# Routing by six digits of the key in place of five, in a fused attention, mixture and expert kernel

## The chip, the cores and the metric

The kernel runs on one core of one Trainium2 chip. The metric is the device time of one execution in microseconds (us); lower is better. A core has five engines that run their own instruction queues in order: TensorE (PE in the rows; PEld is its weight loading), VectorE (DVE), ScalarE (ACT), GpSimd (POOL) and SyncE (SP), which issues most of the transfers. They meet at semaphores.

## The reference

Three stages follow each other. The first is windowed attention with four sink keys (4 batches, 8 heads, 768 positions). The second takes the 3072 tokens by 512 features, multiplies them by three weights, takes the largest of the three elementwise, and multiplies by an output weight. The third gives each token to one of eight experts:

```python
cap = N // E                              # 3072 // 8 = 384
logits = x @ w_gate                       # [3072, 8]
order = np.argsort(-logits.flatten())
for idx in order:                         # greedy, best bid first
    tok, e = (int(idx) // E, int(idx) % E)
    if assigned[tok] >= 0 or counts[e] >= cap:
        continue
    assigned[tok] = e
    counts[e] += 1
for e in range(E):
    mask = assigned == e
    out[mask] = np.maximum(x[mask] @ w1[e], 0.0) @ w2[e]
```

## The kernel before

Attention and the second stage run in eight groups of 384 tokens, and the second stage's matmuls (L295, L317) fill TensorE to about 665 us. Then the eight experts are computed one after another, in the order in which the routing closes them: each has 96 matmuls of 384 columns for the first layer (L604, hidden tile `mm`) and 72 of 512 columns for the second (L597, `acc`). Every weight is split into a high and a low part first: ScalarE copies the high part (L549, `wah`, `wbh`), VectorE or GpSimd subtracts for the low one (L551, `wbl`, `wal`). L608 does the same for the hidden activations on VectorE (`hl`).

Routing is the class `Route`. The greedy loop is done in at most seven phases: in each phase every unassigned token bids for its best open expert, and the phase ends when one expert becomes full. It looks for the bid value at which that happens. The bids become 32-bit integer keys whose order is that of the bids (L418, L419), and the value is found digit by digit, from the top, with a tree of counts. `SH` holds the shift of each digit and `NZ` the number of values that it can have. One pass of the loop below is called a level here.

```python
for l in range(n):
    k=s.NZ[l]
    if l==0: pc=s.pc
    else:
        pc=s.ps.tile([128,512],FT,name="rc")
        s.count(pc,s.compare(z,k,OP.is_ge),k)
    w=s.t([128,24],FT,"w")
    if l<n-1: V.scalar_tensor_tensor(w,z[:,:,0],128.0,DS[:,l,:],op0=OP.mult,op1=OP.add)
    V.tensor_scalar(met[0:M,0:k],pc[0:M,0:k],s.RP[0:M],None,op0=OP.is_ge)
    nc.tensor.matmul(v[:,0:k],s.scale[0:M],met[0:M,0:k],start=True,stop=True)
    V.tensor_scalar(hit[:,1:k],v[:,1:k],128.0,None,op0=OP.min,op1=OP.add,accum_out=d)
    V.tensor_scalar(z,w[:,:,None].to_broadcast([128,24,2]),d,None,op0=OP.subtract)
```

`compare` (L398, tile `th`) holds the digit of each of the 3072 tokens (24 columns on 128 partitions) against the k thresholds, 24 times k results in bf16 on VectorE. `count` (L404) sums them per expert on TensorE: 24 matmuls, each with its own 128x128 weight load from the one-hot bids (`ohr`) and k moving columns. `met` (L448) asks which counts exceed the expert's room, one matmul with `scaleb` (L450) spreads that over all partitions, `hit` (L451) adds up the digit, and `z` (L453) keeps of each token what decides the next digit. A level thus goes from VectorE to TensorE, back, to TensorE again and back. The first level's compare belongs to `bids` (L422); the other digits are cut out of the key there too (L430 to L432).

After the levels come the choice of the expert (L455 to L487), a rank over the tokens (L493, L494) and `slots`, which makes the list of tokens of the expert that was closed: a compare `th` from `ub`, a small product `vt` (L522), and 24 matmuls of six columns (L526), from which the indices `idx` come (L529). GpSimd then gathers the 384 rows from memory (L562, `xg`), and TensorE transposes them (L25 on `pt`; for the first expert L578 and L580) before that expert starts. `turn` emits these transposes inside the expert before.

A scheduler places every instruction into its engine's queue at build time. Step n+2 of the routing and its gather carry a raised priority and are spread over the matmuls of expert n (`s2`); step 0 lies among the last second-stage matmuls and step 1 at the start of the first expert (`s1`). What stands in TensorE's queue behind a routing matmul waits until that one's operand is there.

Of the kernel before, what the change touches and what calls it, by code (L numbers as in the profile page):

```python
# [26 lines left out]
class Attn:  # L27
    def __init__(s, tc, q,k,v, keep, consts, pst, psp, pss, psv, work):
        s.tc=tc; s.nc=nc=tc.nc; s.q,s.k,s.v=q,k,v
        s.pst,s.psp,s.pss,s.psv,s.w=pst,psp,pss,psv,work  # L30
        jp=work.tile([128,128],I32,name="jp",tag="qs0",bufs=2)
        nc.gpsimd.iota(jp,pattern=[[1,128]],base=0,channel_multiplier=-1)
        s.ident=keep.tile([128,128],FR,name="ident")
        nc.vector.tensor_scalar(s.ident,jp,0.0,None,op0=OP.is_equal)
        s.ca=consts.tile([128,2,128],U8,name="ca")
        nc.vector.tensor_scalar(s.ca[:,0,:],jp,0.0,None,op0=OP.is_le)
        nc.vector.tensor_scalar(s.ca[:,1,:],jp,0.0,None,op0=OP.is_gt)
        s.ul=consts.tile([128,2,128],BF,name="ul")
        nc.vector.tensor_scalar(s.ul[:,0,:],jp,0.0,None,op0=OP.is_lt)
        nc.vector.tensor_scalar(s.ul[:,1,:],jp,0.0,None,op0=OP.is_ge)  # L40
        s.negs=consts.tile([128,2,4],FT,name="negs"); nc.vector.memset(s.negs,NEG)

        s.ps=consts.tile([128,160],FR,name="psn"); nc.vector.memset(f32(s.ps),0.0)
        s.vn=consts.tile([16,2,64],FT,name="vns"); nc.vector.memset(s.vn,0.0)
        s.vk=[]
        for i in range(2):
            t=consts.tile([128,2,128],FR,name=f"vk{i}"); nc.vector.memset(f32(t),0.0); s.vk.append(t)
        s.ks=consts.tile([128,2,64],FT,name="kss"); nc.vector.memset(s.ks,0.0)
        s.kf=[]; s.kz=[s.zeros([consts.tile([128,4,132],FR,name=f"kz{h}") for h in range(2)])]
        t=consts.tile([1,1],FT,name="one"); nc.vector.memset(t,0.0)  # L50
        nc.scalar.activation(t,t,AF.Exp)
        s.n=0; s.no=('kh0','kh1'); s.early=[]
        s.extra=None
        s.acc=lambda u: False
# [298 lines left out]
class Route:  # L353

    SH=(25,18,12,6,0); NZ=(128,128,64,64,64)
    M=128
    def __init__(s,tc,LG,pool,work,ps,cap=384):
        s.tc=tc; s.nc=nc=tc.nc; s.LG=LG; s.w=work; s.ps=ps; s.cap=cap  # L360
        c=pool; n=len(s.SH); V=nc.vector
        io=work.tile([128,192],FT,name="te")[:,0:128]
        nc.gpsimd.iota(io,pattern=[[1,128]],base=0,channel_multiplier=0,allow_small_or_imprecise_dtypes=True)
        s.thr=c.tile([128,128],BF,name="thr")
        V.tensor_copy(s.thr,io)
        pi=c.tile([128,1],FT,name="pcol"); s.pcol=pi
        nc.gpsimd.iota(pi,pattern=[[0,1]],base=0,channel_multiplier=1,allow_small_or_imprecise_dtypes=True)
        s.ones=c.tile([128,128],BF,name="onesb"); V.memset(s.ones,1.0)
        s.scale=c.tile([128,128],BF,name="scaleb"); V.memset(s.scale,128.0*8/s.M)
        s.tri=c.tile([128,128],BF,name="trib")  # L370
        V.tensor_scalar(s.tri,io,pi,1.0,op0=OP.is_ge,op1=OP.subtract)
        s.rank8=c.tile([128,8],FT,name="rank8")
        V.tensor_scalar(s.rank8,io[:,0:8],-1.0,8.0,op0=OP.mult,op1=OP.add)
        s.io8=c.tile([128,8],FT,name="io8"); V.tensor_copy(s.io8,io[:,0:8])
        s.io3=c.tile([128,3],FT,name="io3"); V.tensor_copy(s.io3,io[:,0:3])
        s.cp=c.tile([128,24,2],FT,name="cp")
        V.tensor_copy(s.cp[:,:,0],pi.to_broadcast([128,24]))
        V.tensor_copy(s.cp[:,:,1],io[:,0:24])

        po=c.tile([128,1],I32,name="pown"); pf=c.tile([128,1],FT,name="pownf")  # L380
        V.tensor_copy(po,pi); V.tensor_scalar(po,po,7,None,op0=OP.bitwise_and); V.tensor_copy(pf,po)
        s.own=c.tile([128,8],FT,name="own"); V.tensor_scalar(s.own,s.io8,pf,None,op0=OP.is_equal)
        s.sh=c.tile([128,n-1,24],I32,name="shifts"); s.mk=c.tile([128,n-1,24],I32,name="masks"); s.z24=c.tile([128,24],FT,name="z24"); V.memset(s.z24,0.0)
        for l in range(1,n):
            V.memset(s.sh[:,l-1,:],s.SH[l])
            V.memset(s.mk[:,l-1,:],127 if s.NZ[l]==128 else 63)
        s.R=c.tile([128,8],FT,name="room"); V.memset(s.R,float(cap))
        s.RP=c.tile([128,1],FT,name="roomp"); V.memset(s.RP,float(cap))
        s.UA=c.tile([128,24],FT,name="taken"); V.memset(s.UA,0.0)
        s.ASG=c.tile([128,24,8],BF,name="asg"); V.memset(s.ASG,0.0)  # L390
        s.ML=c.tile([128,24,8],FT,name="ml")
# [13 lines left out]
    def bids(s,r=(0,24),first=False):  # L405

        nc=s.nc; n=len(s.SH); V=nc.vector; a,b=r; m=b-a; C=slice(a,b)
        if a==0:
# [10 lines left out]
        V.tensor_tensor(key,key,bid.bitcast(I32),op=OP.bitwise_xor)  # L419
        V.tensor_scalar(s.D0[:,C],key,s.SH[0],s.NZ[0]-1,op0=OP.logical_shift_right,op1=OP.bitwise_and)  # L420
        V.tensor_copy(s.z[:,C],s.D0[:,C][:,:,None].to_broadcast([128,m,2]))
# [11 lines left out]
    def phase(s,bids=True):  # L433
        nc=s.nc; n=len(s.SH); V=nc.vector; M=s.M
        if bids: s.bids()
# [310 lines left out]
```

## Time and profile before

| | before |
|---|---|
| device time, three runs | 1047.61, 1052.06, 1052.12 us; median 1052.06 |
| the profiled execution's own time | 1053.32 us |
| span of its trace | 1051.5 us |
| TensorE busy | 978.9 us (93% of the span) |
| VectorE busy | 774.3 us (74%) |
| ScalarE, GpSimd busy | 512.4 us (49%), 414.5 us (39%) |

The span runs from the first to the last recorded instruction; 1.8 us of the execution's time lie around it. Busy time of TensorE is that of overlapping matmuls, so two neighbours' starts tell what one costs. Where a row names a releaser, an engine stood idle until that instruction was done.

### The profile page before, as it was taken

The numbers are of one execution on the slowest core, as the hardware profiler recorded it, in microseconds if no ns is written. First come the engines' busy times: TensorE is split into PE (matmuls) and PEld (weight loads), VectorE is DVE, ScalarE is ACT, GpSimd is POOL, SyncE is SP. The second block draws the span as 40 slices with busy tenths as digits, with TensorE's granted clock in tenths as the row PEclk, the third lists the DMA queues.
The fourth block names the chain that finished last, engine by engine and source line by source line (L and its number), as shares of the span: only waits on it lengthen the run. The fifth ranks groups of instructions, "written<-read, shape, count | busy, mean of one in ns | idle before, by whom it ended". The sixth has DMA issues, their size and how long they took to land. (4 is left out here: it accounts for less than half of the span.)

```text
span 1051.5 us, 18670 instructions
## 1 busy us (share of the span) xinstructions
PE 978.9 (93%) x6682; PEld 893.3 (85%) x6682; DVE 774.3 (74%) x1822; ACT 512.4 (49%) x1166; POOL 414.5 (39%) x355
## 2 busy tenths in 40 slices
PE   6889999989999999999999999898978999899997
PEld 4658789989999999999999898777767778688896
DVE  6789976688888888988976526877868888763330
ACT  5775563577666666666664211423323333344441
POOL 2666635234444434444344000415334254272431
PEclk8899999999999999999999999989999999999999
DMA  5564421231121121122110000424234253364530
GB/s 136 132 169 138 141 58 49 70 100 46 42 56 47 45 71 41 39 70 46 42 41 2 1 1 31 148 83 146 91 110 153 71 160 102 120 207 119 156 100 31
DMA packets 148845, 89.61 MB, mean 85 GB/s; under 512 B 90160, under 2 KB 133680, under 8 KB 148752
## 3 DMA queue, kind: packets, MB, share of 16 engines
q1 hardware_dynamic: 144048, 74.39, 25.4%
q0 software_dynamic: 3840, 12.45, 3.6%
q10 hardware_dynamic: 864, 1.57, 0.4%
q8 instruction: 53, 0.87, 0.3%
q14 instruction: 40, 0.33, 0.1%
HBM read 74.76 MB, written 13.76 MB: 84 GB/s over the span
## 5 line engine op out<-in xcount | busy, mean ns | idle before, releaser
L551 POOL TENSOR_TENSOR wal<-sa,wah 128x512 fp32r<-128x512 f32 x64 | 89.1, 1393 | 204.1 <-ACT wah L549 198.3
L202 POOL TENSOR_TENSOR L<-A_w,H 128x768 fp32r<-128x768 f32 x46 | 87.2, 1895 | 140.2 <-ACT H L201 121.0
L317 PE MATMUL mm<-woh,hh 128*128 128x260 f32 (+1 forms) x288 | 83.3, 292 | 2.2 <-DVE LG L320 1.1
L549 ACT ACTIVATE wah<-sa 128x512 fp32r<-128x512 f32 x64 | 40.4, 631 | 91.6 <-PE mm L604 50.4
L317 PE MATMUL mm<-woh,hl 128*128 128x260 f32 (+1 forms) x288 | 82.4, 290 | 2.4 <-DVE hl L334 1.2
L317 PE MATMUL mm<-wol,hh 128*128 128x260 f32 (+1 forms) x288 | 82.3, 287 | 0.0
L298 DVE TENSOR_TENSOR hm<-mm,hm 128x384 f32<-128x384 f32 x96 | 53.1, 553 | 37.7 <-PE mm L295 36.7
L597 PE MATMUL acc<-wbl,hh 128*128 128x512 f32 x192 | 78.3, 408 | 0.0
L597 PE MATMUL acc<-wbh,hh 128*128 128x512 f32 x192 | 78.0, 406 | 0.1
L597 PE MATMUL acc<-wbh,hl 128*128 128x512 f32 x192 | 78.0, 406 | 0.0
L551 DVE TENSOR_TENSOR wbl<-sb,wbh 128x512 fp32r<-128x512 f32 x64 | 52.2, 818 | 32.8 <-ACT wbh L549 31.4
L549 ACT ACTIVATE wbh<-sb 128x512 fp32r<-128x512 f32 x64 | 40.3, 630 | 68.0 <-PE acc L597 55.7
L608 DVE SCALAR_TENSOR_TENSOR hl<-mm,hh 128x384 fp32r<-128x384 f32 x64 | 35.4, 554 | 50.9 <-ACT hh L607 47.6
L295 PE MATMUL mm<-xh,w0h 128*128 128x384 f32 x192 | 67.8, 353 | 2.3 <-DVE hm L298 1.1
L295 PE MATMUL mm<-xh,w1h 128*128 128x384 f32 x192 | 66.7, 347 | 1.7 <-DVE hm L298 0.9
L295 PE MATMUL mm<-xl,w0h 128*128 128x384 f32 x192 | 65.8, 342 | 0.8 <-DVE xl L285 0.8
L295 PE MATMUL mm<-xh,w2h 128*128 128x384 f32 x192 | 66.0, 344 | 0.3 <-ACT hm L297 0.3
L295 PE MATMUL mm<-xh,w2l 128*128 128x384 f32 x192 | 65.1, 339 | 0.0
L295 PE MATMUL mm<-xh,w1l 128*128 128x384 f32 x192 | 65.0, 338 | 0.0
L295 PE MATMUL mm<-xl,w1h 128*128 128x384 f32 x192 | 64.9, 338 | 0.0
L295 PE MATMUL mm<-xh,w0l 128*128 128x384 f32 x192 | 64.9, 338 | 0.0
L295 PE MATMUL mm<-xl,w2h 128*128 128x384 f32 x192 | 64.8, 338 | 0.0
(334 smaller groups left out, 3156.7 us busy)
## 6 DMA issues: line engine op xcount, KB each, us to landing
sa<-in_moe_w_dram SPq DMA_DIRECT2D x64, 256.0 KB
sb<-in_moe_w_dram SPq DMA_DIRECT2D x64, 256.0 KB
st<-in_moe_w_dram SPq DMA_DIRECT2D x18, 512.0 KB
qn<-in_q_dram SPq DMA_DIRECT2D x60, 96.0 KB
x2d<-xo SPq DMA_DIRECT2D x18, 256.0 KB
kn<-in_k_dram SPq DMA_DIRECT2D x32, 128.0 KB
st<-in_moe_w_out_dram SPq DMA_DIRECT2D x6, 512.0 KB
vn<-in_v_dram SPq DMA_DIRECT2D x24, 128.0 KB
```

Of the source, the lines that this page charges most:

```text
L202: nc.gpsimd.tensor_tensor(L,Af,f32(H),op=OP.subtract)
L295: nc.tensor.matmul(ps[:,:384],s.W[i][a][:,p,f*128:(f+1)*128],X[p][b],start=(n==0),stop=(n==11)); n+=1
L298: else: nc.vector.tensor_tensor(m,ps[:,:384],m,op=OP.max)
L317: nc.tensor.matmul(ps[:,:n],H[f][a][:,t*128:(t+1)*128],s.WO[b][:,f,u,:n],start=(k==0),stop=(k==17)); k+=1
L549: nc.scalar.activation(h,src,AF.Copy)
L551: (nc.vector if s.cv%2==0 else nc.gpsimd).tensor_tensor(l,src,f32(h),op=OP.subtract)
L597: nc.tensor.matmul(acc[t],H[f][a][:,t*128:(t+1)*128],W[f][1][b],start=(f==0 and n==0),stop=(f==F-1 and n==2)); n+=1
L608: nc.vector.scalar_tensor_tensor(l,ps[:,:384],0.0,f32(h),op0=OP.max,op1=OP.subtract)
```

## The change

The 32 bits of the key are cut into six digits of 6, 6, 5, 5, 5 and 5 bits in place of five of 7, 7, 6, 6 and 6. The masks are worked out from `NZ` in the same way for every digit. All other code stays.

```diff
-    SH=(25,18,12,6,0); NZ=(128,128,64,64,64)
+    SH=(26,20,15,10,5,0); NZ=(64,64,32,32,32,32)
...
-            V.memset(s.mk[:,l-1,:],127 if s.NZ[l]==128 else 63)
+            V.memset(s.mk[:,l-1,:],s.NZ[l]-1)
```

So a phase has six levels, with 64, 64, 32, 32, 32 and 32 thresholds. On VectorE the first phase (step 0) shows it. Before, the rows from the second level's compare on are these; each level is th, w, met, hit, z:

```order
L398 TENSOR_TENSOR th<-z,thr 128x3072
L444 SCALAR_TENSOR_TENSOR w<-z,digs 128x24
L448 TENSOR_SCALAR met<-rc,roomp 128x128
L451 TENSOR_SCALAR hit,digit<-rc 128x127
L453 TENSOR_SCALAR z<-w,digit 128x48
L398 TENSOR_TENSOR th<-z,thr 128x24x64
L444 SCALAR_TENSOR_TENSOR w<-z,digs 128x24
L448 TENSOR_SCALAR met<-rc,roomp 128x64
```

Now, at the same place:

```order
L398 TENSOR_TENSOR th<-z,thr 128x24x64
L444 SCALAR_TENSOR_TENSOR w<-z,digs 128x24
L448 TENSOR_SCALAR met<-rc,roomp 128x64
L451 TENSOR_SCALAR hit,digit<-rc 128x63
L453 TENSOR_SCALAR z<-w,digit 128x48
L398 TENSOR_TENSOR th<-z,thr 128x24x32
L444 SCALAR_TENSOR_TENSOR w<-z,digs 128x24
L448 TENSOR_SCALAR met<-rc,roomp 128x32
```

The instructions of a level are the same and narrower, and one more level of them follows behind.

The second place is TensorE's queue inside the second expert, from the last of step 2's six-column matmuls (L526) to the first transposes of the third expert's rows (L25); the L404 are counts of step 3. Before, 13 L597, 12 L604 and one count of 24 stand between them:

```order
L526 MATMUL rc<-vt,th 128x6
L597 MATMUL acc_9864<-wbh,hl_9959 128x512
...
L597 MATMUL acc_9863<-wbh,hh_9996 128x512
L404 LDWEIGHTS ohr
L404 MATMUL rc<-th,ohr 128x128
...
L450 MATMUL rc<-met,scaleb 128x128
...
L597 MATMUL acc_9865<-wbh,hl_9997 128x512
L25 MATMUL pt<-ident,xg 128x128 x3
```

Now 18 L597, 22 L604 and three counts (64, 64 and 32 columns) stand there:

```order
L526 MATMUL rc<-vt,th 128x6
L604 MATMUL mm<-hh_9486,wal 128x384
...
L404 MATMUL rc<-th,ohr 128x64
...
L450 MATMUL rc<-met,scaleb 128x64
...
L597 MATMUL acc_10018<-wbh,hh_10150 128x512
L404 LDWEIGHTS ohr
L404 MATMUL rc<-th,ohr 128x32
...
L25 MATMUL pt<-ident,xg 128x128 x3
```

The transposes moved behind two more counts and 15 more expert matmuls. For the second expert's rows it is the other way round: between the last L526 of step 1 and the first L25 stood 6 L604, 8 L597 and a count of 128 columns, and now stand 5 L604, 6 L597 and a count of 64.

## Rows read from the trace of the kernel before

**Rows 1.** Busy time by stage: window, length, each engine's us (instructions), TensorE clock, DMA.
```profile
665.00:700.00 35.00, 29.40 (x247) 27.06 (x248) 27.70 (x63) 11.80 (x28) 13.16 (x10) 0.85 0.40 122
...
sum 308.00, PE 276.08 PEld 237.81 DVE 247.84 ACT 99.23 POOL 112.42; mean PE 34.51 PEld 29.73 DVE 30.98 ACT 12.40 POOL 14.05
```

**Rows 2.** Chain that ended last, inside the sixth expert: start, us, engine, count.
```profile
944.15 2.09 PE acc L597 x9
946.25 2.08 PE mm L604 x12
```

**Rows 3.** TensorE's waits, 632 to 940 us: total us, times, longest.
```profile
PE rc L450 <- DVE met L448: 10.4, 7, 3.4
PE pt L25 <- DMA xg<-x2d,idx: 6.2, 5, 2.7
PE rc L526 <- DVE vt L522: 5.5, 7, 2.3
PE rc L404 <- DVE th L398: 3.5, 3, 1.9
...
PE rc L404 <- DVE ohr L428: 1.4, 2, 0.9
```

**Rows 4.** Timeline of TensorE, 757 to 782 us: start, us, operation, count, idle before.
```profile
758.17 0.74 PE L526 MATMUL rc<-vt,th 128*128 128x6 bf16 x24 [0.53 <-DVE vt L522]
758.78 0.48 PE L597 MATMUL acc<-wbh,hl 128*128 128x512 f32 x1
...
762.84 1.51 PE L404 MATMUL rc<-th,ohr 128*128 128x128 bf16 x24 [0.53 <-DVE ohr L428]
764.16 0.48 PE L597 MATMUL acc<-wbl,hh 128*128 128x512 f32 x1
...
769.18 0.33 PE L25 MATMUL pt<-ident,xg 128*128 128x128 f32 x1 [2.67 <-DMA xg<-x2d,idx]
771.55 0.48 PE L25 MATMUL pt<-ident,xg 128*128 128x128 f32 x1 [2.04 <-DMA xg<-x2d,idx]
...
778.94 0.87 PE L404 MATMUL rc<-th,ohr 128*128 128x64 bf16 x24
779.65 0.48 PE L597 MATMUL acc<-wbh,hh 128*128 128x512 f32 x1
```

**Rows 5.** VectorE's routing groups by form: count, busy us, mean ns, idle before.
```profile
L398 DVE TENSOR_TENSOR th<-z,thr 128x3072 bf16<-128x3072 bf16 x13 | 25.0, 1921 | 0.2
L398 DVE TENSOR_TENSOR th<-z,thr 128x1536 bf16<-128x1536 bf16 x21 | 21.3, 1013 | 0.6
L398 DVE TENSOR_TENSOR th<-z,thr 128x384 bf16<-128x384 bf16 x1 | 0.4, 352 | 0.0
L453 DVE TENSOR_SCALAR z<-w,digit 128x48 bf16<-128x48 f32 x35 | 12.0, 343 | 1.0
L444 DVE SCALAR_TENSOR_TENSOR w<-z,digs 128x24 f32<-128x24 bf16 x28 | 7.8, 279 | 0.0
L448 DVE TENSOR_SCALAR met<-rc,roomp 128x64 bf16<-128x64 f32 x21 | 5.9, 279 | 8.2 <-PE rc L404 6.3 <-remote 1.9
L448 DVE TENSOR_SCALAR met<-rc,roomp 128x128 bf16<-128x128 f32 x14 | 4.8, 344 | 6.1 <-PE rc L404 5.8
L451 DVE TENSOR_SCALAR_CACHE_REDUCE hit<-rc 128x63 bf16<-128x63 f32 x21 | 4.7, 223 | 7.3 <-PE rc L450 7.3
L451 DVE TENSOR_SCALAR_CACHE_REDUCE hit<-rc 128x127 bf16<-128x127 f32 x14 | 4.1, 289 | 6.2 <-PE rc L450 6.2
L451 DVE DVE_READ_ACCUMULATOR hit<-rc 128x1 f32 x35 | 2.9, 83 | 0.0
```

**Rows 6.** Busy time in the first expert's step 1, columns as in rows 1.
```profile
672.00:684.00 12.00, 9.00 (x88) 8.65 (x86) 11.72 (x23) 4.49 (x10) 4.70 (x4) 0.95 0.50 159
```

**Rows 7.** Timeline of VectorE, then of TensorE, around step 1's gather.
```profile
714.87 2.85 DVE L398 TENSOR_TENSOR th<-z,thr 128x3072 bf16<-128x3072 bf16 x1
...
727.45 0.33 PE L25 MATMUL pt<-ident,xg 128*128 128x128 f32 x1 [0.49 <-DMA xg<-x2d,idx]
```

## The prediction, made before the changed kernel was run

> **What bounds the kernel now.** I looked at busy time by stage first, since routing runs only from 600 us on. From 632 to 940 us, where all routing phases but the first half of step 0 lie, TensorE is busy 276 of 308 us and VectorE 248 [rows 1]: TensorE sets the time, and some 32 us of it are lost in waits. After 940 us the routing is over and the chain that ended last runs through matmuls back to back, 0.232 us for one of the second layer and 0.173 us for one of the first [rows 2]. So the change can act in two ways only: by the TensorE time that routing itself takes, and by TensorE's waits inside the experts. The table of TensorE's waits says for whom it waited [rows 3]: 10.4 us for met before L450, 3.5 us for a compare before a count, 1.4 us for ohr before a count, 5.5 us for vt before L526, and 6.2 us for gathered rows. The first three belong to the levels: 15.3 us over 35 levels (five in each of seven phases), 0.44 us a level. Idle time of VectorE costs nothing by itself; VectorE counts where TensorE stands behind it.
>
> **TensorE's own work.** A count's price is the distance from its start to the next matmul's. With 128 columns it is 762.84 to 764.16, 1.32 us; with 64, 778.94 to 779.65, 0.71 us; the 24 six-column matmuls with the same kind of weight load take 758.17 to 758.78, 0.61 us [rows 4]. So width pays from 128 to 64, and below that a floor of about 25 ns a matmul is near. For 32 columns I take the middle of the two last, 0.66. A phase had 2 x 1.32 + 3 x 0.71 = 4.77 us of counts and gets 2 x 0.71 + 4 x 0.66 = 4.06; the added L450, one narrow matmul, takes about 0.05 (0.03 is what one of the 64-column count takes). That is 0.66 us less a phase, 4.6 us less in seven. With 32 columns at 0.61 it would be 6.0, at 0.71 it would be 3.2; 32 columns cannot cost half of 64, since six don't.
>
> The Trainium skill, "TensorE: Matmul & The Clock Gate", section "Back-to-back issue gap", gives one price of about 60 cycles, 25 ns, for every width from 1 to 64 columns, and 134 cycles for 128; by it the narrowing from 64 to 32 would bring TensorE nothing at all, which speaks against the change. The rows differ at 64 (0.71 us is 29.6 ns each, not 25) and agree at six. By the page the sum would be 2 x 1.34 + 3 x 0.60 before and 6 x 0.60 after, 0.83 less a phase with the added matmul, 5.8 in all against my 4.6; the measured 64 decides.
>
> **VectorE's work.** Means by form [rows 5]: a compare takes 1.92 us with 128 thresholds and 1.01 with 64; for 32 (768 results a partition) the line through 384 results (0.35) and 1536 (1.01) gives 0.57. Narrowing saves 2 x 0.91 + 3 x 0.44 = 3.14 us a phase, and met and hit 0.07 each in the two levels that had 128, 0.26 together (what they gain from 64 to 32 I leave out). The added level costs w 0.28, th 0.57, met 0.28, hit 0.22, its read 0.08 and z 0.34, 1.77 in all. Net 1.6 us less a phase; cutting out one more digit is a row's edge in three short instructions and is not counted. Over the six phases inside the experts that is some 10 us of VectorE time. What of it reaches TensorE is between nothing and all of it. Two places show where it does:
>
> Step 1, 672 to 684 us: VectorE is busy 11.72 of 12 us, TensorE 9.00 [rows 6]. There VectorE is the bound, and the compares of the first two levels stand ahead of what TensorE waits for: 2 x 0.91 us plus 0.13, **1.9 us less**.
>
> The wait before L526 in step 1's slots, the longest of its kind at 2.3 us [rows 3]: ahead of vt stands the next step's first compare, which took 2.85 us there [rows 7]. With 64 thresholds it takes 1.01, and 1.9 us at most come back; since TensorE arrives a little earlier too, I take **1.3 less**, with 0 and 1.9 as bounds.
>
> The rest of VectorE's relief I give no value.
>
> **The added round trip.** Each phase has one more place where TensorE can stand before L404 and L450. Behind the waiting matmul in the queue are the expert's own (L597, L604), and nobody else can run them. At the mean of 0.44 us a level, seven levels cost **3.1 us more**. The lower bound is 0 (the scheduler leaves expert matmuls between a count and its L450, and between that and the next count). The upper bound comes from the waits that did occur before L450 and after th: 13.9 us in 10 times, 1.39 each; one such wait in every added level is 9.7 us.
>
> **The gathers.** For the third expert TensorE waited 2.67 and 2.04 us, 4.7 together, for gathered rows [rows 4]. Between the last L526, from which the indices come, and the first transpose stood 13 x 0.232 + 12 x 0.173 + 1.32 = 6.4 us; now there are 18 x 0.232 + 22 x 0.173 + 0.71 + 0.71 + 0.66 = 10.1. The 3.6 us between them is work that TensorE has to do anyway, so that much of the wait goes: **3.6 less**, about 1.1 left. Bounds: nothing (the gather is late by as much, because the issue on GpSimd is) and 4.7. For the second expert's rows the same count of the queue gives 6 x 0.173 + 8 x 0.232 + 1.32 = 4.2 us before and 5 x 0.173 + 6 x 0.232 + 0.71 = 3.0 after. TensorE waited there already, 0.49 us for the first tile [rows 7], so the lost 1.2 us are added: **1.2 more** (0 if the indices come earlier by as much).
>
> **What costs nothing.** Step 0's levels lie among second-stage matmuls that TensorE does meanwhile; their narrower counts are in the 4.6 us. Two more constants are set before, where VectorE has room.
>
> **The sum.** Less 4.6, 1.9, 1.3 and 3.6, more 3.1 and 1.2: 7.1 us less. The profiled execution took 1053.3 us, so 1046.2. The median of the three runs lies 1.3 lower, at 1052.06; I say 1046.
>
> **The rivals.**
> *The round trips eat the gain.* If the seven added levels take one full wait of 1.39 us each (9.7) and only the 4.6 us of counts and half of the other gains (3.4) come back, less the 1.2 of the second expert, the time is 1053.3 - 4.6 - 3.4 + 1.2 + 9.7 = 1056. With a wait half as long it is 1051. For it: TensorE did wait 10 times in 35 levels, 1.39 us in the mean. Against: the queue keeps the same three to five matmuls between count and L450.
> *Slower.* One mechanism: the added level's L450 or next count is placed where VectorE is behind by a weight split whose weights came late; the longest of such waits is 3.4 us [rows 3]. Priced at the three phases of six that would have it, 3 x 3.4 = 10.2, on top of the mean 3.1 and with the counts' 4.6 alone on the other side, it gives 1062. It is slower by over 0.5% (5.3 us) from 1057.3 on, that is, once the added levels cost 8.6 us, 1.23 each. For it: VectorE is busy 248 of 308 us. Against: it gets less to do.
> *VectorE's relief spreads.* If it returns half of its 10 us in place of the 3.2 that I counted, and the round trips cost nothing, the time is 1053.3 - 4.6 - 5.0 - 3.6 + 1.2 = 1041.
> *No effect.* The queue shows that the counts are narrower and one more, so the change does what it says; that all of it hides is part of the first rival.
>
> **How the numbers follow.** The forecast (1042 to 1049) has 0.45, the spread relief (1037 to 1042) 0.12, the eaten gain (1049 to 1057) 0.31, slower 0.12. Runs of this kernel lie within some 5 us of each other, so 0.5% is about what can be told from no change. Faster by more than that means below 1046.8: the spread relief and some three quarters of the forecast, 0.46. Slower means above 1057.3, 0.12; the rest, 0.42, is within 0.5%. The range reaches from 1039 to 1056: below it lie the lower part of the spread relief, above it the slower case and the end of the eaten gain, 2 in 10 together.
>
> **What would show it.** A count of 32 columns from start to next start: 0.61 to 0.71 us right, 0.35 or 1.3 wrong. The mean of the compare with 768 results: 0.57. TensorE's busy time summed from 632 to 940 us should fall with the span, and the waits before L450 and before L404 together should be 15 to 19 us in 42 levels; over 25 would be the rival. The wait for the third expert's gathered rows should be near 1 us in place of 4.7, the second expert's up to 1.2 longer. The prediction is wrong above all if waits appear at other places, since every step of the routing is dealt out anew among the expert's matmuls and their weights' arrival.

## The result, and the profile after

The changed kernel takes 1035.64 us in the median of four runs (1031.47 to 1040.72), the kernel before 1050.82 in four. The ratio is 0.9875 with a 95% interval of 0.9838 to 0.9912: some 13 us less, where 7 were forecast, and below the range.

The page of the profiled execution (1031.47 us, the fastest of the four), its span and its engines:

```profile
span 1029.7 us, 19074 instructions
...
PE 964.8 (94%) x6857; PEld 878.4 (85%) x6857; DVE 756.8 (73%) x1866; ACT 511.5 (50%) x1166; POOL 409.2 (40%) x355
```

The two spans differ by 21.8 us, more than the 13 to 15 of the runs. 6.4 us of that arise before the first routing instruction, in code that is the same but for constants: the transpose of the seventh group's output (L25 on `mm`) begins at 592.92 us now and began at 599.29. From there to the eighth group's, the last, 0.7 us come in; step 0's first count lies there. The rest of this section speaks of what follows the start of that last transpose, 626.50 now and 633.61 before: 409.7 us before, 395.0 now, 14.7 less.

TensorE's waits from 632 to 940 us, which answer to [rows 3] (total us, times, longest):

```profile
PE rc L526 <- DVE vt L522: 7.2, 6, 3.6
PE rc L450 <- DVE met L448: 5.5, 6, 1.4
PE rc L404 <- DVE th L398: 3.9, 6, 1.0
PE acc L580 <- DMA xg<-x2d,idx: 3.8, 2, 2.9
...
PE pt L25 <- DVE xl L584: 0.6, 1, 0.6
PE pt L25 <- DMA xg<-x2d,idx: 0.3, 1, 0.3
```

With seven levels more, the waits for met and for a compare are 9.4 us in place of 13.9. The gathered rows of the later experts are hardly waited for, 0.3 us in place of 6.2. Longer are above all vt before L526 (7.2 for 5.5) and the first expert's gathered rows (3.8 for nothing).

Busy time by stage, columns as in [rows 1]; the third number from the end is TensorE's granted clock:

```profile
672.00:684.00 12.00, 11.24 (x122) 10.32 (x120) 8.29 (x23) 4.94 (x10) 4.54 (x4) 0.92 0.51 155
696.00:708.00 12.00, 9.86 (x51) 8.52 (x50) 11.95 (x34) 4.92 (x9) 5.20 (x4) 1.00 0.48 154
632.00:940.00 308.00, 282.11 (x2513) 241.38 (x2513) 232.03 (x772) 108.11 (x211) 115.38 (x90) 0.98 0.41 127
...
630.00:665.00 35.00, 33.53 (x390) 32.11 (x390) 24.77 (x107) 9.79 (x28) 7.44 (x5) 0.96 0.26 86
665.00:700.00 35.00, 29.20 (x256) 25.23 (x256) 27.17 (x94) 11.01 (x22) 8.46 (x8) 0.95 0.39 122
700.00:740.00 40.00, 34.18 (x309) 27.99 (x308) 32.87 (x94) 13.86 (x26) 17.60 (x14) 0.91 0.41 127
...
780.00:820.00 40.00, 37.71 (x336) 31.66 (x335) 32.04 (x106) 13.24 (x25) 15.02 (x12) 0.96 0.43 133
```

VectorE is busy 232 of 308 us where it was 248. TensorE's busy time from 632 to 940 us went up, from 276 to 282, where the prediction wanted a fall: in a fixed window the experts' matmuls take the place of the routing that is over sooner. In 672 to 684 us, where VectorE had been the bound with 11.72 of 12, it is busy 8.29 and TensorE 11.24; but everything begins some 7 us earlier now, so this window holds other work. In windows of 12 us over step 1's levels, from 665 to 692 us, VectorE is busy 7.0 to 10.1 now. It is full behind them, in the slots (696 to 708). The four stretches left out (740 to 780, and 820 to 940) have a clock of 1.00; in the kernel before the eight read 1.00, 0.85, 0.96, 0.91, 0.96, 1.00, 0.97 and 0.99. A granted clock of 0.85 over 35 us is 5.3 us that TensorE does not have at full speed. Summed in this way in pieces of 10 us, the clock costs 13.6 us before and 8.5 now. It is an upper value, since part of it lies in waits, and it differs from execution to execution. Over the whole span the mean granted clock was 0.977 in the profiled execution of the kernel before and 0.981 in the mean of 76 others; in the changed kernel it was 0.985 and, in the mean of its four, 0.984. By these means the clock costs 20 us before and 17 now, so its part in the gain is likelier 3.5 us than 5.

The chain that ended last runs at the end as in [rows 2], matmul behind matmul at the same price (start, us, engine, count):

```profile
944.75 2.08 PE acc L597 x9
946.83 2.12 PE mm L604 x12
```

So the gain lies in the stretch with routing. From each kernel's timeline of TensorE, from that transpose to the last matmul, I added up start-to-start times of the counts and the idle times by what ended them, and put the clock's loss beside them. The last column tells how long the routing took inside the experts, from step 0's first L526 to step 6's. The remainder of the first column without counts, idle and clock is 329 to 332 us in all of these, as it should be, since the experts' matmuls are the same:

| us | whole stretch | counts | all idle | of it L450 and L404 | L526 | gathered rows | clock | routing |
|---|---|---|---|---|---|---|---|---|
| before | 409.7 | 32.9 | 30.9 | 15.3 | 5.5 | 6.2 | 13.6 | 260.4 |
| after | 395.0 | 27.9 | 26.5 | 10.3 | 7.2 | 4.2 | 8.5 | 240.6 |
| e1, wide compares | 408.8 | 28.1 | 34.0 | 9.8 | 5.3 | 16.4 | 15.4 | 274.0 |
| e2, wide counts | 401.4 | 40.3 | 21.7 | 9.3 | 8.6 | 0.0 | 8.5 | 238.9 |
| e3, both wide | 417.1 | 41.6 | 31.5 | 8.5 | 4.4 | 14.0 | 15.3 | 277.0 |
| e4, five levels | 396.9 | 22.5 | 33.7 | 12.3 | 8.2 | 4.4 | 8.5 | 234.5 |
| e14, VectorE loaded | 406.9 | 28.0 | 32.8 | 15.6 | 5.5 | 4.2 | 15.3 | 259.5 |
| e15, VectorE relieved | 400.3 | 33.6 | 29.0 | 10.9 | 5.3 | 3.2 | 6.8 | 241.9 |

By this account the change's 14.7 us are 5.0 of counts, 4.4 of waits and 5.1 of clock. Each row is one execution: that of the kernel before took 2.5 us more than its median, the changed kernel's 4.2 less, and e14's 4.3 more.

How a wait costs more than its own length is seen in step 1's slots. TensorE's timeline, columns as in [rows 4]:

```profile
705.46 0.40 PE L597 MATMUL acc<-wbh,hl 128*128 128x512 f32 x1
709.44 0.17 PE L526 MATMUL rc<-vt,th 128*128 128x6 bf16 x1 [3.58 <-DVE vt L522]
...
712.60 0.63 PE L597 MATMUL acc<-wbh,hl 128*128 128x512 f32 x1
713.03 0.63 PE L597 MATMUL acc<-wbh,hh 128*128 128x512 f32 x1
...
718.87 0.33 PE L25 MATMUL pt<-ident,xg 128*128 128x128 f32 x1 [0.33 <-DMA xg<-x2d,idx]
...
721.58 0.77 PE L404 MATMUL rc<-th,ohr 128*128 128x32 bf16 x24
722.20 0.42 PE L604 MATMUL mm<-xh,wah 128*128 128x384 f32 x1
...
765.35 0.52 PE L25 MATMUL pt<-ident,xg 128*128 128x128 f32 x3 [0.56 <-DVE xl L584]
```

And the granted clock around that wait, in windows of 2 us:

```profile
706.00:708.00 2.00, 0.00 (x0) 0.10 (x1) 2.00 (x3) 0.63 (x1) 1.28 (x2) 1.00 0.23 69
708.00:710.00 2.00, 0.56 (x12) 0.56 (x12) 2.00 (x4) 0.00 (x0) 1.22 (x1) 0.50 0.00 0
...
716.00:718.00 2.00, 2.00 (x21) 1.76 (x21) 1.40 (x6) 0.16 (x1) 0.00 (x0) 1.00 0.76 240
```

TensorE stood still for 3.58 us, then the granted clock is 0.50, the level of 1.2 GHz, and it is back at 1.00 from 716 us on. In between a matmul of 512 columns takes 0.43 us from start to start (712.60 to 713.03) in place of 0.232. The same rows hold two steps of the prediction: a count of 32 columns takes 0.62 us (721.58 to 722.20), and the third expert's transpose at 765.35 waits no more for the gather but 0.56 us for VectorE.

VectorE's groups by form, which answer to [rows 5]:

```profile
L398 DVE TENSOR_TENSOR th<-z,thr 128x768 bf16<-128x768 bf16 x28 | 18.2, 649 | 0.8
L453 DVE TENSOR_SCALAR z<-w,digit 128x48 bf16<-128x48 f32 x42 | 15.6, 372 | 1.3
...
L398 DVE TENSOR_TENSOR th<-z,thr 128x1536 bf16<-128x1536 bf16 x13 | 13.5, 1037 | 0.2
L448 DVE TENSOR_SCALAR met<-rc,roomp 128x32 bf16<-128x32 f32 x28 | 6.9, 246 | 6.6 <-PE rc L404 6.6
...
L444 DVE SCALAR_TENSOR_TENSOR w<-z,digs 128x24 f32<-128x24 bf16 x35 | 6.2, 176 | 0.0
```

The compares take 32.7 us with two pieces that are not shown (0.8 and 0.2), where they took 48.3 (pieces of 1.6 and 0.4 included).

### The profile page after: what moved, and what is told of

It is laid out like the page before. It is cut to its first block, busy times and chain, and to the rows that moved or that the text cites. A ratio compares the mean times of both kernels' runs of the same rounds, so it can differ in the third digit from the quotient of the medians.

```text
span 1029.7 us, 19074 instructions
## 1 busy us (share of the span) xinstructions
PE 964.8 (94%) x6857; PEld 878.4 (85%) x6857; DVE 756.8 (73%) x1866; ACT 511.5 (50%) x1166; POOL 409.2 (40%) x355
## 4 chain that ended last, share of the span: by engine, by line
PE 54%; DVE 25%; issue 6%; DMA 6%; ACT 5%; POOL 2%; SPq 0%; POOLq 0%; DVEq 0%; ACTq 0%
PE mm L295 22%; PE mm L604 7%; PE acc L597 7%; PE mm L317 4%; PE po L206 2%; DMA sa<-in_moe_w_dram 2%; PE pt L25 2%; DMA st<-in_moe_w_dram 2%; PE rc L404 2%; DVE th L398 2%; DVE cA L250 2%; DVE A_w L188 1%; PE pp L25 1%; PE ps L142 1%; DVE hl L608 1%
## 5 line engine op out<-in xcount | busy, mean ns | idle before, releaser
L549 ACT ACTIVATE wah<-sa 128x512 fp32r<-128x512 f32 x64 | 40.4, 631 | 84.4 <-PE mm L604 44.5
L597 PE MATMUL acc<-wbh,hl 128*128 128x512 f32 x192 | 78.5, 409 | 0.2 <-DVE hl L608 0.2
L597 PE MATMUL acc<-wbl,hh 128*128 128x512 f32 x192 | 78.5, 409 | 0.0
L597 PE MATMUL acc<-wbh,hh 128*128 128x512 f32 x192 | 78.2, 407 | 0.0
L549 ACT ACTIVATE wbh<-sb 128x512 fp32r<-128x512 f32 x64 | 40.3, 630 | 75.4 <-PE acc L597 66.5
L551 DVE TENSOR_TENSOR wbl<-sb,wbh 128x512 fp32r<-128x512 f32 x64 | 45.6, 714 | 31.5 <-ACT wbh L549 31.0
## 6 DMA issues: line engine op xcount, KB each, us to landing
sa<-in_moe_w_dram SPq DMA_DIRECT2D x64, 256.0 KB
sb<-in_moe_w_dram SPq DMA_DIRECT2D x64, 256.0 KB
x2d<-xo SPq DMA_DIRECT2D x18, 256.0 KB
```

Of the source, the lines that this page charges most:

```text
L549: nc.scalar.activation(h,src,AF.Copy)
L551: (nc.vector if s.cv%2==0 else nc.gpsimd).tensor_tensor(l,src,f32(h),op=OP.subtract)
L597: nc.tensor.matmul(acc[t],H[f][a][:,t*128:(t+1)*128],W[f][1][b],start=(f==0 and n==0),stop=(f==F-1 and n==2)); n+=1
```

## The experiments

All ratios are to the kernel before, with a 95% interval. The theory to be tested: what brought the gain is VectorE's relief, nearly all of it that of the narrower compares (A in the expectations). The rivals: the narrower counts on TensorE, and the new deal of the queue, that is, where the scheduler happens to put the routing's instructions.

**The change taken apart: e1, e2, e3, e4.** e1 keeps the six levels and the narrow counts, and makes each compare twice as wide (128, 128, 64, 64, 64 and 64 thresholds); the additional results are not counted.

```diff
-    SH=(26,20,15,10,5,0); NZ=(64,64,32,32,32,32)
+    SH=(26,20,15,10,5,0); NZ=(64,64,32,32,32,32); KW=(128,128,64,64,64,64)
-        s.compare(s.z,s.NZ[0],OP.is_ge,s.TH,r)
+        s.compare(s.z,s.KW[0],OP.is_ge,s.TH,r)
-                s.count(pc,s.compare(z,k,OP.is_ge),k)
+                s.count(pc,s.compare(z,s.KW[l],OP.is_ge),k)
```

> The changed kernel with VectorE's compares at twice the thresholds (128, 128, 64, 64, 64, 64), of which the counts read the first half; counts, met and hit stay narrow. It undoes the narrowing on VectorE alone and keeps the sixth level: some 3.2 us more VectorE time a phase. Theory A (the gain is VectorE's shorter chain: fewer waits of TensorE, and fewer stretches at the low clock behind them): most of the gain goes, ratio to before 0.997 to 1.010; waits before L450 and L404 back to 15 us or more. Theory B (the gain is the accident of a new order of the queues): another new order, anywhere from 0.985 to 1.005 without relation to the widths. Theory C (TensorE's narrower counts are the gain): 0.985 to 0.990, as the changed kernel.

Measured: 1051.18 us, 1.0015 (0.9986 to 1.0043). The whole gain is gone, with TensorE's narrow counts still there (28.1 us). TensorE's waits from 600 us on show where the lateness came out:

```profile
PE pt L25 <- DMA xg<-x2d,idx: 11.5, 9, 2.0
PE rc L526 <- DVE vt L522: 5.3, 5, 2.3
PE acc L580 <- DMA xg<-x2d,idx: 4.8, 2, 3.8
```

The levels themselves wait no longer than in the changed kernel, 9.8 us before L450 and L404 where A expected 15 or more: the ratio is as A said, the place of the waits is not. The routing as a whole ends later (the last count lies 291.6 us behind the stretch's start, 256.0 in the changed kernel, 275.1 before), so the gathers are late, and the transposes that depend on them. A late end has no fixed price: e1 ends 16.5 us behind the kernel before and takes the same time, with 4.8 us less of counts.

e2 keeps the narrow compares and lets each count stream its columns twice:

```diff
-            s.nc.tensor.matmul(pc[0:s.M,0:k],s.OHR[:,c],TH[:,c,0:k],start=(c==0),stop=(c==23))
+            s.nc.tensor.matmul(pc[0:s.M,0:2*k].rearrange('p (r k) -> p r k',r=2),s.OHR[:,c],TH[:,c,None,0:k].to_broadcast([128,2,k]),start=(c==0),stop=(c==23))
```

> The changed kernel with every count streaming its columns twice (128, 128, 64, 64, 64, 64 columns of the same narrow compare, the second half unused). It undoes the narrowing on TensorE alone: 2 x (1.32 - 0.71) + 4 x (0.71 - 0.60) = 1.7 us a phase, 11.6 us in seven, of which those in a wait cost nothing. Theory A: 4 to 12 us above the changed kernel, ratio to before 0.990 to 0.998, with waits before L450 and L404 as short as in the changed kernel or shorter, about 10 us. Theory B: anywhere from 0.985 to 1.005. Theory C: all of the gain goes, 0.998 or more.

Measured: 1040.19, 0.9938 (0.9906 to 0.9970). That is in A's range and outside the one by which the narrower counts are the gain. The counts cost 12.4 us more of TensorE's time, and about half of that is lost in the result.

e3 has both wide, that is, a sixth level and nothing narrower:

```diff
-        s.count(s.pc,s.TH,s.NZ[0],r)
+        s.count(s.pc,s.TH,s.KW[0],r)
-            k=s.NZ[l]
+            k=s.KW[l]
```

> The changed kernel's six digits with compares, counts, met and hit at 128, 128, 64, 64, 64, 64 thresholds: the sixth level alone, without the narrowing. A sixth level at 64 costs by the rows of before 0.71 us of TensorE and 2.2 us of VectorE a phase. Theory A: slower than before, ratio 1.005 to 1.020, waits before L450 and L404 above 15 us. Theory B: 0.990 to 1.010. Theory C: 1.003 to 1.006, the seven counts alone.

Measured: 1057.94, 1.0070 (1.0038 to 1.0103). The ratio is in A's range; the waits before L450 and L404, 8.5 us, are not above 15 as A expected. Now the four kernels with six levels give both parts twice. Narrower compares: from e3 to e2 1.3%, from e1 to the changed kernel 1.4%. Narrower counts: from e3 to e1 0.55%, from e2 to the changed kernel 0.6%. In the steps from e3 met and hit get narrower too, 3.8 us of VectorE. The sixth level at the old widths: 0.7% the other way. Of 1050 us that is -14, -6 and +7. These add up to the measured 13 less by construction, since each step starts where another ends; that the two ways agree is one comparison. The runs leave each step uncertain by about half a per cent, and each has a deal of the queue of its own. So the compares' part is clear of that, the counts' part hardly.

e4 has the narrow widths and five levels; the lowest five bits of the key are left out:

```diff
-    SH=(26,20,15,10,5,0); NZ=(64,64,32,32,32,32)
+    SH=(26,20,15,10,5); NZ=(64,64,32,32,32)
```

> The changed kernel without its last level: five digits of 6, 6, 5, 5 and 5 bits, which leaves out the lowest five bits of the key, so bids that agree in the upper 27 bits are taken as equal. What the sixth level costs is the distance to the changed kernel. Theory A: a level takes 0.6 us of TensorE and about 1.8 us of VectorE a phase, so 4 us for sure and up to 17 if VectorE's part reaches TensorE as it did in the change; ratio to before 0.971 to 0.984. If the round trip itself is what costs (1.39 us of wait a level), 0.974. Theory B: 0.980 to 1.000, without relation to the level.

Measured: 1036.51, 0.9878 (0.9852 to 0.9903), the same as the changed kernel, outside A's range (0.971 to 0.984) and inside B's. VectorE's compares take 27.4 us in place of 32.7, and the routing 234.5 in place of 240.6, yet the time is the same: TensorE has 5.4 us less of counts and 7.2 us more of waits. So in this deal the level that is missing was no cost. Why the waits grew by as much was not settled.

**The deal of the queue: e5, e6, e7, e8.** Each edit moves some VectorE instructions in the code and changes nothing in what they compute, so that the scheduler deals out the queue anew. e5 (changed kernel) and e7 (before) move the expert's number to the head of `slots`; e6 and e8 move the five one-hot instructions of `bids` ahead of the key.

```diff
@@ slots, moved from its end to its head
+        V.tensor_tensor_reduce(d,E1,s.io8,1.0,0.0,op0=OP.mult,op1=OP.add,accum_out=ef)
+        V.tensor_copy(ei,ef)
@@ bids, moved ahead of the key (first and last of five)
+        V.tensor_tensor(eq,ML,bid[:,:,None].to_broadcast([128,m,8]),op=OP.is_equal)
+        if s.M>8: V.tensor_copy(s.OHR[:,C].rearrange("p c (r e) -> p c r e",e=8),s.OH[:,C,None,:].to_broadcast([128,m,s.M//8,8]))
```

> The changed kernel with the two short instructions that give the expert's number written at the head of the slots in place of their end: the same work, but the scheduler deals the queues anew (some 500 rows differ on VectorE). Theory A (the narrower compares on VectorE bring the gain, by what TensorE waits for and by the clock behind the waits, in any order): ratio to before 0.982 to 0.993. Theory B (the gain is the accident of one order): 0.99 to 1.005, and the two kernels of either width overlap.

> The changed kernel with the one-hot of the bids written ahead of the key in place of behind it: the same work in another order (some 640 rows differ on VectorE). Theory A: 0.982 to 0.993. Theory B: 0.99 to 1.005.

> The kernel before with the same rewriting as in the first of these runs (expert's number first). Theory A: 0.995 to 1.006, above both of the changed kernel's. Theory B: 0.985 to 1.005.

> The kernel before with the one-hot ahead of the key. Theory A: 0.995 to 1.006, above both of the changed kernel's. Theory B: 0.985 to 1.005.

Measured: e5 1039.27, 0.9904 (0.9872 to 0.9936); e6 1032.02, 0.9829 (0.9774 to 0.9884); e7 1050.22, 0.9993 (0.9963 to 1.0023); e8 1039.28, 0.9891 (0.9838 to 0.9944). Such an edit alone can be worth 1.1%, almost as much as the change. e8 is outside A's range and inside B's, and as fast as e5 (1039.3 us both), so kernels of the two widths do overlap when the deal differs, as B said; e5 and e7 lie in both ranges, e6 in A's alone. But within each pair the change makes it faster, and in no pair do the times of the runs overlap: 0.9904 to 0.9993 is 0.991, 0.9829 to 0.9891 is 0.994, and the plain pair is 0.9875.

**One place later: e9, e10, e13.** The next expert's transposes begin one hidden tile later. e9 is this edit in the kernel before, e10 in the changed one, e13 in e6.

```diff
-            if f==5 and mid is not None: mid()
+            if f==6 and mid is not None: mid()
```

> The kernel before with the transposes of the next expert's rows written into the present expert at its seventh hidden block in place of its sixth, so that they stand later in TensorE's queue; widths and levels as before. If what the wide compares cost comes through late indices and so through waits for gathered rows (6.2 us in the trace of before, and the clock behind them), this brings part of the change's gain without it: ratio 0.985 to 0.994, waits for gathered rows under 2 us. If lateness only moves to the next thing that TensorE needs (the waits before L450, L404, L526 grow by as much): 0.995 to 1.005.

> The changed kernel with the same later transposes. Its trace has 4.2 us of waits for gathered rows, 3.8 of them for the first expert, which this edit does not move; so there is little to gain: 0.983 to 0.990 by the theory of late indices, and 0.985 to 0.997 if a new deal of the queues is all that it is.

> The changed kernel with the one-hot ahead of the key and the later transposes together, the two edits with the lowest ratios (0.983 and 0.981). If the edits add: 0.976 to 0.981. If each was a new deal of the queues and no more: 0.980 to 0.992.

Measured: e9 1049.14, 0.9960 (0.9936 to 0.9983); e10 1035.90, 0.9810 (0.9771 to 0.9850), a fourth pair with 0.985; e13 1029.93, 0.9838 (0.9799 to 0.9876). e9 is in the range for lateness that only moves, and 0.4% faster. e10 is below both of its ranges. e13 is in the range for new deals and above that for edits that add. e6, e10 and e13 are the fastest kernels of this study and can't be told apart. TensorE's waits of e9 from 600 us on, beside [rows 3]:

```profile
PE rc L450 <- DVE met L448: 11.6, 10, 3.0
PE rc L526 <- DVE vt L522: 7.5, 6, 3.3
PE rc L404 <- DVE th L398: 6.2, 4, 2.9
...
PE pt L25 <- DMA xg<-x2d,idx: 1.8, 2, 1.5
```

The wait for gathered rows fell from 6.2 to 1.8 us, as the edit meant, and these others grew by 1.2, 2.0, 2.7 and, for ohr (2.8 now), 1.4, together 7.3. All idle time went from 30.9 to 32.4 us. So the wait that was cured here came back elsewhere; the last count lies 271.1 us behind the stretch's start, 275.1 before. That it came back because the routing is still late was not shown: waits shift by as much in a new deal alone (e7 waits 11.6 us for gathered rows).

**Seven levels: e11.** From the kernel before, with still narrower digits:

```diff
-    SH=(25,18,12,6,0); NZ=(128,128,64,64,64)
+    SH=(27,22,17,12,8,4,0); NZ=(32,32,32,32,16,16,16)
-            V.memset(s.mk[:,l-1,:],127 if s.NZ[l]==128 else 63)
+            V.memset(s.mk[:,l-1,:],s.NZ[l]-1)
```

> Seven digits of 5, 5, 5, 5, 4, 4 and 4 bits: 32, 32, 32, 32, 16, 16, 16 thresholds. One step further the same way. Counts at the floor of 0.61 us: seven of them 4.3 us a phase against 2 x 0.73 + 4 x 0.60 = 3.9 now. VectorE: compares 4 x 0.65 + 3 x 0.40 = 3.8 against 2 x 1.04 + 4 x 0.65 = 4.7, and one more set of small instructions, 1.0 us. So TensorE gets 0.4 us a phase more and VectorE the same: no further gain, ratio to before 0.986 to 0.995. A rival by which every narrowing of the compare pays: below 0.982; one by which each level's round trip costs its 1.39 us: 0.995 or more.

Measured: 1047.94, 0.9946 (0.9908 to 0.9983). It gives back over half of the gain, at the upper end of what was expected. Its compares take 27.3 us, less than with six levels (32.7), but its routing 263.3, more than before the change. Its counts take 29.6 us, more than with six levels, and its profiled execution, 6.6 us above its median, shows 20.5 us of clock's loss against 8.5.

**VectorE's load away from the routing: e14, e15, e12.** If VectorE is a second bound of the stage, its load must tell wherever it lies. e14 gives it four more instructions an expert in the changed kernel, whose output nobody reads:

```diff
+        if f%2==1:
+            dm=s.wp.tile([128,512],BF,name="dm",bufs=1)
+            nc.vector.tensor_tensor(dm,b,b,op=OP.subtract)
```

> The changed kernel with four more VectorE instructions in each expert (512 elements of a weight subtracted from themselves into a scratch tile that nobody reads), about 0.7 to 0.8 us each, some 3 us an expert: as much VectorE time as the wide compares take, off the routing's chain. Theory load: the gain of the narrowing goes, ratio to before 0.995 to 1.003. Theory chain: 0.985 to 0.992.

Measured: 1045.82, 0.9966 (0.9949 to 0.9984): three quarters of the gain are gone. They take 0.947 us in the mean, 32 of them, 30.3 us; 22 of them, 20.7 us, lie ahead of the last L526. TensorE's waits of e14 from 600 us on:

```profile
PE rc L450 <- DVE met L448: 7.7, 5, 3.5
PE rc L526 <- DVE vt L522: 5.5, 7, 2.4
PE rc L404 <- DVE th L398: 5.4, 3, 2.5
PE pt L25 <- DMA xg<-x2d,idx: 4.2, 3, 1.7
```

No matmul waits for dm itself. TensorE waits for the same routing instructions as before the change, 15.6 us before L450 and L404 with the 2.5 us for ohr. dm does more than keep VectorE busy: up to the last L526 VectorE also stands idle before it for 6.8 us until the weights have landed, with the routing's instructions behind it in the queue.

e15 is the other way round: in the kernel before, half of VectorE's splits of the second weights are left out, and with them the low parts of those blocks, for which an earlier block's low part is used.

```diff
+            if s.cv%4==0:
+                r.append((h,s.pl)); continue
+            l=s.wp.tile(list(src.shape),FR,name=nm+"l",bufs=s.nring); s.pl=l if nm=="wb" else getattr(s,"pl",None)
```

> The kernel before with four of the eight low weight parts that VectorE computes in each expert left out; the second layer's matmuls of these blocks read the low part of the block before, so TensorE does the same matmuls on other data. VectorE has 3.5 us less to do in an expert (4 x 0.87), about what the narrow compares take from it, all of it off the routing's chain. Theory load: ratio 0.982 to 0.992. Theory chain: 0.996 to 1.004.

Measured: 1041.36, 0.9919 (0.9894 to 0.9944). Without any edit to the routing, two thirds of the gain are there, and the waits and the clock read like the changed kernel's: 10.9 us before L450 and L404, and 6.8 us of clock.

Both ratios are as the theory of load has them, but each differs from its kernel by less than e8's edit without meaning, 1.1%. The length of the routing tells more. These are step 0's and step 6's first L526 in the kernel before, the changed kernel, e14 and e15:

```profile
663.68 0.74 PE L526 MATMUL rc<-vt,th 128*128 128x6 bf16 x24 [0.48 <-DVE vt L522]
924.07 0.74 PE L526 MATMUL rc<-vt,th 128*128 128x6 bf16 x24 [0.27 <-DVE vt L522]
...
657.07 0.74 PE L526 MATMUL rc<-vt,th 128*128 128x6 bf16 x24 [0.73 <-DVE vt L522]
897.65 0.42 PE L526 MATMUL rc<-vt,th 128*128 128x6 bf16 x11
...
662.20 0.74 PE L526 MATMUL rc<-vt,th 128*128 128x6 bf16 x24 [0.58 <-DVE vt L522]
921.71 0.52 PE L526 MATMUL rc<-vt,th 128*128 128x6 bf16 x15 [0.76 <-DVE vt L522]
...
661.45 0.69 PE L526 MATMUL rc<-vt,th 128*128 128x6 bf16 x22 [0.49 <-DVE vt L522]
903.31 0.74 PE L526 MATMUL rc<-vt,th 128*128 128x6 bf16 x24
```

From one to the other it is 260.4, 240.6, 259.5 and 241.9 us. The four deals at the old widths (before, e7, e8, e9) take 260.4, 258.4, 249.0 and 256.3; the five at the new ones (after, e5, e6, e10, e13) 240.6, 245.8, 240.8, 242.2 and 236.3, without an overlap. e1 and e3, with the wide compares and six levels, take 274.0 and 277.0. e14 has the new widths and lies among the old ones, e15 the other way round. So VectorE's load sets how fast the routing goes, on its chain or off it: e14 and e15 move it by 18.9 and 18.5 us, the deals by 11.4 at most. From the routing's length to the time is a looser step: over the 17 traces the length and the whole stretch go together with a correlation of 0.89, and e4 has the shortest routing without being the fastest.

e12 had tried this by giving two of VectorE's eight splits an expert to GpSimd in the kernel before:

```diff
-            (nc.vector if s.cv%2==0 else nc.gpsimd).tensor_tensor(l,src,f32(h),op=OP.subtract)
+            (nc.vector if s.cv%2==0 and s.cv%16 not in (4,12) else nc.gpsimd).tensor_tensor(l,src,f32(h),op=OP.subtract)
```

> The kernel before with two of the eight weight splits that VectorE does in each expert given to GpSimd: 1.7 us less VectorE work an expert (2 x 0.87), 2.9 us more on GpSimd, nothing of the routing changed. Theory load (TensorE waits because VectorE has too much to do, whatever it is): the gain of VectorE's relief comes here too, ratio 0.988 to 0.996. Theory chain (only the routing's own steps count, since TensorE waits for these): 0.997 to 1.005, or worse if GpSimd becomes late.

Measured: 1055.24, 1.0091 (1.0050 to 1.0131), above both ranges; the theory of the chain had left room for "worse if GpSimd becomes late". GpSimd takes 1.39 us for such a subtraction where VectorE takes 0.77, and it also issues the gathers; which of the two made it slower was not tried. Nor was VectorE relieved: from the eighth group's transpose on it is busy 275.0 us in e12 and 277.8 before, and the routing takes 259.8 us as before. So e12 decides nothing.

## Why the prediction was wrong

**The step that failed** is "The rest of VectorE's relief I give no value". Two places were priced, 1.9 and 1.3 us, as if VectorE counted only where TensorE stood behind it by name. In its place the runs show that the narrower compares were worth 14 us (e3 to e2, there with met and hit, and e1 to after alone). VectorE's compares take 52.6 us in e1 from 590 us on (27.8, 23.0, 1.5 and 0.3) and 32.7 in the changed kernel, 56.1 in e3 and 30.2 in e2: each of these 19.9 and 25.9 us returned 0.7 and 0.5 us. Off the routing chain, counted up to the last L526, e14 lost 0.9% or 9.5 us for 20.7 us added, 0.46 each, and e15 gained 0.8% or 8.5 us for 21.3 us taken away (wbl 36.8 us before, 15.5 in e15), 0.40 each. Each of these prices carries what the deal may add or take, up to 11 us (e8), so the two on the chain and the two off it can't be told apart; and e4 took 5.3 us of compares away and got nothing back. What does stand clear of the deal is that VectorE's load lengthens or shortens the routing, by some 20 us here. Every one of steps 1 to 6 but one is shorter in the changed kernel (52.4, 36.1, 39.3, 35.8, 38.7 and 38.3 us from L526 to L526; 55.4, 39.1, 45.4, 40.2, 38.4 and 41.8 before), since the routing goes from TensorE to VectorE and back in every level. TensorE's waits and the clock behind them, 44.5 us in sum, left room enough; what the prediction lacked was a price for making the whole chain earlier.

The rival that was nearest, "VectorE's relief spreads", gave 1041 from a profiled execution of 1053.3; 0.9875 of that is 1040.1. The measured median, 1035.64, lies below even its band of 1037 to 1042. Its chance of 0.12 was too low, and its half of the relief was less than what came back.

**The clock** had no term. A wait was priced by its length, though [rows 1] showed a clock of 0.85 in a stretch where TensorE was busy 29.4 of 35 us. 5.1 of the 14.7 us are clock in the profiled executions, some 3.5 over the whole span by the means of all runs. So "in two ways only" left out a third.

**The counts.** Forecast 4.6 less, measured 5.0. A count of 32 columns takes 0.60 to 0.62 us where nothing disturbs it, at the lower end of what was given, by which the prediction's sum is 6.0. Counts at the low clock take longer (709.47 to 710.72 for one of 64 columns, 1.25 us), so that the two sums lie so near is partly luck. The Trainium skill, "TensorE: Matmul & The Clock Gate", section "Back-to-back issue gap", has one price of 25 ns for 1 to 64 columns: 0.60 us over 24 is 25.0 ns, so at 32 columns the traces agree; at 64 they show 0.71 us again (29.6 ns each), so the narrowing from 64 to 32 was worth something here.

**VectorE's prices.** The compare with 768 results was put at 0.57 us and takes 0.649 in the mean (0.558 in e14). Undisturbed it takes 0.54 to 0.56, so the price was right; what lifts the mean is told in the last section.

**The added round trip**, 3.1 us. At the old widths a sixth level costs 7 us (e3). Its trace has 8.7 us more of counts and 0.6 more of idle time, with the waits before L450 and L404 down from 15.3 to 8.5, so the term isn't seen there either. At the new widths the level costs nothing that can be seen (e4), and the waits before L450 and L404 fell to 10.3 us in 42 levels, 0.25 each, where 15 to 19 us were forecast. The price of a round trip was taken from the kernel before, as if it did not depend on how late VectorE is.

**Step 1's stretch**, 1.9 less. VectorE has room in step 1's levels now, 7.0 to 10.1 of 12 us. From step 0's first L526 to the first L493 behind step 1's levels it is 37.3 us now and was 40.2, 2.9 less, of which 0.7 are narrower counts; so the size was about right. That VectorE was the only reason was not shown.

**The wait before L526 in step 1**, 1.3 less, went the other way: 3.58 us where it was 2.3, at the end of a stretch in which VectorE is busy 11.95 of 12 us. The compare ahead of vt has half the results, but the row in the last section shows it at 2.02 us, and vt at 1.41 where it had taken 0.90.

**The gathers.** The third expert's wait went from 4.7 to none for the gather and 0.56 us for the split, so that "3.6 less" was right and somewhat low. The second expert's was to grow by 1.2 and is 0.33 us, where it had been 1.5 in three waits; the indices came earlier, one of the bounds. The first expert's 3.8 us were not foreseen.

**The deal.** What was said last, that waits may appear at other places since everything is dealt out anew, holds. Four pairs give 0.9875, 0.991, 0.994 and 0.985 for the change; the mean is 0.989. The change is worth about 1.1%, give or take half a per cent by the deal. What makes one deal better than another was not settled.

## What to carry to other kernels

Where a chain of short instructions goes back and forth between two engines and the second is about three quarters busy, price what is taken off that second engine even where no wait names it: here 0.4 to 0.7 us came back for each microsecond, on the chain or off it, by four comparisons that each carry the deal, and nothing in a fifth (e4). A wait cured at one place can come back at the next, so that moving a consumer (0.4% here) may be worth less than shortening the chain. And before a change of 1% in such a schedule is believed or dropped, time it in two or three deals of the queue, since an edit without any meaning moved this kernel by 1.1%.

## What the runs showed that was not expected

**VectorE and GpSimd get in each other's way.** VectorE's rows of the changed kernel (columns as in [rows 7]):

```profile
680.72 0.54 DVE L398 TENSOR_TENSOR th<-z,thr 128x768 bf16<-128x768 bf16 x1
...
683.27 1.56 DVE L398 TENSOR_TENSOR th<-z,thr 128x768 bf16<-128x768 bf16 x1
...
706.04 2.02 DVE L398 TENSOR_TENSOR th<-z,thr 128x1536 bf16<-128x1536 bf16 x1
707.98 1.41 DVE L522 TENSOR_TENSOR vt<-ve,cp 128x144 bf16<-128x144 f32 x1
```

And GpSimd's at the same times:

```profile
683.13 1.28 POOL L551 TENSOR_TENSOR wal<-sa,wah 128x512 fp32r<-128x512 f32 x1 [2.98 <-ACT wah L549]
...
705.06 2.18 POOL L551 TENSOR_TENSOR wal<-sa,wah 128x512 fp32r<-128x512 f32 x1 [1.00 <-ACT wah L549]
707.96 1.26 POOL L551 TENSOR_TENSOR wal<-sa,wah 128x512 fp32r<-128x512 f32 x1 [0.72 <-ACT wah L549]
```

Of the 28 compares of this form, 25 take 0.54 to 0.56 us. The other three are those that begin inside a subtraction of GpSimd: 1.19 us (675.91), 1.56 (683.27) and 1.53 (727.01). The one of 680.72 takes 0.54 us with GpSimd idle, that of 683.27 takes 1.56 beginning inside GpSimd's subtraction, which ends at 684.41: 0.54 behind that end is 684.95, and the compare ends at 684.83. The compare of 706.04 and vt of 707.98 likewise begin inside a subtraction or just behind its start, and take 1.0 and 0.9 us more than their kind (1.04 in the mean of the changed kernel, and 0.47 for vt in e14). The Trainium skill, "SBUF — State Buffer", section "Who interferes with whom", says that a VectorE instruction with two inputs in SBUF contends with a GpSimd instruction that reads SBUF, and that the port pair which they share is an exclusive lock; the compares agree. vt ends 0.17 us behind the subtraction, less than it takes alone. It isn't only instructions with two tensors: the five z (L453) that begin inside a subtraction end 0.04 or 0.05 us behind its end, and the longest takes 1.21 us in place of 0.25. With the median of what no subtraction overlaps as the undisturbed time of each form, I estimate from the rows of 590 to 960 us that such waiting makes up some 31 us of VectorE's busy time before and 25 now.

**Unchanged code varies by 7 us.** The eighth group's transpose began between 626.5 and 633.6 us in the 17 profiled executions. In the first 50 us the granted clock was 0.86 before and 0.93 after, with VectorE busy 34.8 and 37.3 us of them.
